# Reordering the stage ahead of the first exponential: dense work, slices and the maxima's rows

## Chip, cores and metric

The kernel runs on one core of one Trainium2 chip. The metric is the device time of one execution in microseconds, lower is better.

## The reference

One transformer block with adaptive layer norm. S is 2048 tokens, D is 512, 32 heads of width 16, F is 1792. All is float32.

```
mod = silu(c) @ w_mod                       # six rows of D: sa ca ga sb cb gb
h = layernorm(x) * (1 + ca) + sa
q, k, v = split(h @ wqkv)                   # 32 heads of 16
x = x + ga * (softmax(q k^T * 16**-0.5) v) @ wo
h = layernorm(x) * (1 + cb) + sb
a = h @ w1 + b1
x = x + gb * (a * tanh(softplus(a))) @ w2   # Mish
```

## The kernel before

**Precision.** A dense product is done three times (`mm3`), with each operand split into a high part and a low part: high by high, and the two mixed ones. A weight slice of `wqkv` is brought in by `slice_load` (an SP transfer into one buffer), then parted by `slice_split`: the high copy on ACT (`hi_copy`, L91), the low difference on POOL (`lo_sub`, L98). Kind 0 is queries, 1 keys, 2 values. Queries and keys come in four slices of 128 columns (eight heads each), values in two of 256.

**Setup.** Layer norm, its transposes and the first slices, in a loop over four blocks of 512 tokens. Its end is `constants()`: zero rows into the scratch of the queries (`qscr<-zer`) and of the values, and `b1`.

**Steps.** What follows is written out as steps t from -20 to 257; PRO is 20. Hooks stand at half-steps h: a hook of h = 2t is emitted at the start of step t, one of h = 2t+1 in its middle. A hook fixes an instruction's place in the order of its own engine or queue, and nothing else: each engine, and SP's DMA queue too, works down its own list in order and stops at the first instruction whose operands are missing.

**Steps -20 to -1** find the score maxima of the first group of four heads (and begin with the second). A step has two `max_pair`s: four half-height products on TensorE (L494) into two banks each of a ring of six, and two reductions on VectorE (L496). After them `whole_units` emits dense products out of a queue of units (`plan`): the values of the remaining token chunks (12 products of 256 columns a chunk), then key and query units of 12 products of 512 columns. A unit is taken when its half-step is at least that of its slice's split plus a margin. `CREDIT` says how many 512-column products a step is given. When the last unit of a plan entry is done, its `fin` orders the split of the slice two entries on and the load of the slice three entries on. A key or query unit ends with a copy to `qf` on ACT (L259), a split on POOL (L95, L98, two buffers) and, two half-steps later, writes to scratch by SP: three for queries (`qscr`, L269), two for keys (`kscr`, L273, L274).

**The maxima's rows.** The group's maxima are complete after step -5. In step -4 `max_rows` transposes them (L509), ACT and VectorE make rows of them (`mh` L511, `mt` L512), and the hook `put` at half-step -6 writes these into the query operand, `qa<-mt` (L518, four transfers). The score products of step 0 need them.

**Other transfers of the stage.** `early_prep` loads six parts of `w1`, POOL splits them, and SP writes them back to scratch (L1393, L1401), one each three half-steps. `load_pair` fetches queries and keys of two heads (L310, L319) at half-steps -22 and -8, `load_v` (L467) the values at -3.

**From step 0 on** a step has four score products (L529), each followed by an exponential on ACT (L532), four maxima products for the next group (L480) with their reductions (L482), up to eight half-height dense products (L136), which steps 0 and 1 have not, and eight products with the values (L547) for the step two back. They share the ring. The feed-forward part runs in the dense slots of later steps.

The functions that the diff touches:

Of the kernel before, what the change touches and what calls it, by code (L numbers as in the profile page):

```python
# [18 lines left out]
def adaln_block(ctx: ExitStack, tc: tile.TileContext, x, wqkv, wo, w1, b1, w2, c, w_mod, out):  # L19
# [8 lines left out]
    TB = 512  # L28
    NB = S // TB
# [3 lines left out]
    T = 16 * NIT  # L33
# [5 lines left out]
    PRO = 16 + LEAD  # L39
    CUT1, CUT2 = (0, 1), (2, 3)  # L40
    LOV = ((1,), (), (1, 3), (1, 3))
    PREP = 4
    CREDIT = 7.5
    HCAP = 10.0

    x = x[0]
# [39 lines left out]
    def dap(t, off, ap):  # L86
        return bass.AP(tensor=t.tensor, offset=t.offset + off, ap=ap)

    def hi_copy(eng, hi, src):
        if eng == "a":  # L90
            nc.scalar.copy(hi, src)  # L91
        elif eng == "v":
            nc.vector.tensor_copy(hi, src)
        else:
            nc.gpsimd.tensor_scalar(hi, src, 1.0, 0.0, op0=ALU.mult, op1=ALU.add)  # L95

    def lo_sub(eng, lo, src, hi):
        (nc.gpsimd if eng == "p" else nc.vector).tensor_sub(lo, src, hi.bitcast(F32))  # L98
# [43 lines left out]
    def pe_run():  # L142
        while pe_queue:
            mm_go(pe_queue.pop(0))
# [57 lines left out]
    def at(h, f):  # L202

        hooks.setdefault(h, []).append(f)
# [9 lines left out]
    pw = qkv.enter_context(tc.tile_pool(name="pp", bufs=1, side="right"))  # L214
# [12 lines left out]
    def slice_load(kind, i, pool=None, lp=None):  # L227
        w = P if kind < 2 else 2 * P
        raw = (pool or qp).tile([P, DK, w], F32, tag="raw" if pool is pw else "wr", name="wr", bufs=2 if lp else 1)
        o = kind * D + i * w  # L230
        nc.sync.dma_start(raw, wqkv[:, o:o + w].rearrange("(k p) m -> p k m", p=P))
        slices[kind, i] = raw

    def slice_split(kind, i, pool=None, eng="p", hi_eng="a"):
        raw = slices[kind, i]
        w = raw.shape[2]
        hi = (pool or qp).tile([P, DK, w], F32R, tag="wh", name="wh", bufs=2)
        lo = (pool or qp).tile([P, DK, w], F32R, tag="wl", name="wl", bufs=2)
        hi_copy(hi_eng, hi, raw)
        lo_sub(eng, lo, raw, hi)  # L240
        slices[kind, i] = (hi, lo)
# [84 lines left out]
    with ExitStack() as es:  # L326
# [5 lines left out]
        def load_x(t):  # L332
            xt = lp.tile([P, D], F32, tag="xt", name="xt", bufs=16)
            nc.sync.dma_start(xt, x[t * P:(t + 1) * P, :])
            xts.append(xt)
# [10 lines left out]
        slice_load(2, 0)  # L346
        for t in range(8, 16):
            load_x(t)
        slice_load(1, 1, pw)
        zer = lp.tile([P, TB], F32, name="zer")  # L350
        nc.gpsimd.memset(zer, 0.0)
        for i in range(NR):
# [12 lines left out]
        def stats_tb(tb):  # L365

            mv = lp.tile([P, 4, 2], F32, tag="ln_mv4", name="ln_mv4", bufs=2)
            rs = rss[tb] = lp.tile([P, 4, 4], F32, tag="ln_rs4", name="ln_rs4", bufs=3)
            for i in range(4):
                st_ = lp.tile([P, 6], F32, tag="ln_st", name="ln_st", bufs=4)  # L370
                nc.vector.bn_stats(out=st_, in_=xts[4 * tb + i])
                nc.vector.bn_aggr(out=mv[:, i, :], in_=st_)
            nc.gpsimd.tensor_scalar(rs[:, 0, :], mv[:, :, 1], 1.0, EPS, op0=ALU.mult, op1=ALU.add)
            nc.gpsimd.tensor_scalar(rs[:, 3, :], mv[:, :, 0], -1.0, 0.0, op0=ALU.mult, op1=ALU.add)
            nc.gpsimd.tensor_tensor(rs[:, 1, :], rs[:, 0, :], nhalf.to_broadcast([P, 4]), op=ALU.pow)
            nc.gpsimd.tensor_mul(rs[:, 2, :], rs[:, 3, :], rs[:, 1, :])

        def apply_tb(tb):
            rs = rss.pop(tb)
            for i in range(4):  # L380
                xt = xts[4 * tb + i]
                nc.scalar.activation(xt, xt, AF.Identity, scale=rs[:, 1, i:i + 1], bias=rs[:, 2, i:i + 1])
# [32 lines left out]
        def constants():  # L415
            for q4 in range(S // TB):
                nc.sync.dma_start(dap(qscr, 48 * S + q4 * TB, [[50 * S, H], [S, 2], [1, TB]]), zer[:64, :])
            nc.sync.dma_start(dap(vscr, VROW - 16, [[VROW, P], [P * VROW, G], [1, 16]]), zer[:, :16 * G])
            nc.sync.dma_start(b1c, b1.rearrange("(f p) -> p f", p=P))

        def unit(fin):
            pe_run()
            fin()

        for tb in range(NB):
            if tb + 2 < NB:
                stats_tb(tb + 2)
            if tb == 0:
                slice_split(2, 0, eng="v")
            parts = []  # L430
            for kind in (1, 0) if tb == 0 else (1,):
                fin = qk_unit(kind, 0, tb, "ring")
                parts.append((pe_queue[2 * DK:], fin))
                del pe_queue[2 * DK:]
                pe_run()
            if tb in (1, 2):
                for kc in (2 * tb - 2, 2 * tb - 1):
                    unit(v_unit(0, kc, "ring"))
            if tb + 1 < NB:
                tr_tb(tb + 1, CUT1)  # L440
            for late, fin in parts:
                pe_queue.extend(late)
                unit(fin)
            if tb + 1 < NB:
                tr_tb(tb + 1, CUT2)
            if tb + 2 < NB:
                apply_tb(tb + 2)
            if tb == 0:
                for pp in range(2):
                    load_q(pp, 48)  # L450
            for pp in range(2):
                load_k(pp, tb)
        constants()
        slice_split(1, 1)


    kq2 = ctx.enter_context(tc.tile_pool(name="kq2", bufs=1))
# [713 lines left out]
    cur = {"left": [], "fin": None, "part": []}  # L1171

    def queue(ready, make):
        units.append((ready, make))
# [22 lines left out]

    def whole_units(h, credit):

        while credit > 0:  # L1200
            if not cur["left"]:
                if not units or h < units[0][0]():
                    return
                cur["tag"] = "acc" if cur.get("tag") == "ms" else "ms"
                cur["fin"] = units.pop(0)[1](cur["tag"])
                cur["left"] = list(pe_queue)
                pe_queue.clear()
            m = cur["left"].pop(0)
            mm_go(m)
            credit -= m[0].shape[-1] / TB  # L1210
            if not cur["left"]:
                at(h + 1, lambda fin=cur["fin"]: fin(h + 1))
                cur["fin"] = None
# [7 lines left out]
    def step(t):  # L1221
# [4 lines left out]
        if t < 0:  # L1226
# [10 lines left out]
            for f in ats.pop(t, []):  # L1237
                f()
            whole_units(2 * t + 1, CREDIT)
            do_specials(2 * t + 1)  # L1240
# [83 lines left out]
    def do_specials(h):  # L1324
        if specials and h >= specials[0][0]():
# [2 lines left out]
            at(h + 1, lambda: fin(h + 1))  # L1328


    plan = [(-PRO, 2, 0, range(4, 16)), (-PRO, 1, 1, range(NB)), (-PRO, 0, 1, (0,)), (-PRO, 1, 2, range(NB)),
            (-PRO, 0, 2, (0,)), (0, 2, 1, range(16)), (0, 1, 3, range(NB)), (0, 0, 3, (0,))]
    plan += [(56, 0, ct, (1, 2, 3)) for ct in range(4)]
    split_at = {0: -2 * PRO - 4, 1: -2 * PRO - 4}

    def planned(i, a, tag):
        _, kind, sl, args = plan[i]
        unit = v_unit(sl, a, tag) if kind == 2 else qk_unit(kind, sl, a, tag)

        def fin(h):  # L1340
            if a == args[-1]:
                if i + 2 < len(plan):
                    d = 4 if h > 0 else 1
                    at(h + d, lambda: slice_split(*plan[i + 2][1:3], hi_eng="p" if h > 0 else "a"))
                    split_at[i + 2] = h + d
                if i + 3 < len(plan):
                    at(h + (7 if h > 0 else 2), lambda: slice_load(*plan[i + 3][1:3]))
            unit(h)
            if (kind, sl, a) == (2, 0, NKC - 1):
                at(max(0, h + 2), lambda: first_mods(max(0, h + 2)))  # L1350
            if i + 1 == len(plan) and a == args[-1]:
                mst["qkv"] = h // 2 + 3
        return fin
# [23 lines left out]
        queue_mod(j)  # L1377
    for i, (t0, _, _, args) in enumerate(plan):
        for a in args:
            queue(lambda i=i, t=t0: max(2 * t, split_at.get(i, 4 * T) + 4), lambda tag, i=i, a=a: planned(i, a, tag))  # L1380

    preps = [(w1scr[f], w1[:, f * P:(f + 1) * P].rearrange("(k p) m -> p k m", p=P), None) for f in range(FT)]
    preps += [(woscr[k], wo[k * P:(k + 1) * P, :], 0) for k in range(DK)]
# [4 lines left out]
    def early_prep(i, h):  # L1388

        scr, src, _ = preps[i]  # L1390
        lo, hi = [ap.tile([P, TB], F32R, tag=f"p{(1, 3, 0, 2)[i % 4]}", name="ep", bufs=4 - i % 4 // 2) for _ in range(2)]
        raw = lo.bitcast(F32)
        nc.sync.dma_start(raw.rearrange("p (k m) -> p k m", m=P), src)  # L1393

        def split():
            hi_copy("p", hi, raw)
            lo_sub("p", lo, raw, hi)

        def put():
            for v, part in enumerate((hi, lo)):  # L1400
                nc.sync.dma_start(scr[:, v, :], part.bitcast(F32))  # L1401

        at(h + 7, split)
        at(h + 10, put)

    for i in range(EARLY):
        at(3 * i - 34, lambda i=i: early_prep(i, 3 * i - 34))

    def start_preps(h, i=EARLY, turn=0, puts=()):

# [24 lines left out]
    for qb in range(NB - 1):  # L1435
        t0 = 32 * G * (qb + 1) + 16
# [15 lines left out]
    t = T + 2  # L1452
# [32 lines left out]
```

## Time and profile before

| | us |
|---|---|
| median of 3 runs | 1699.01 |
| lowest, highest | 1698.46, 1699.34 |
| profiled execution | 1697.49 |
| span of its trace | 1695.7 |
| TensorE busy in the span | 1672.8 |
| steps -20 to -1 begin | 50.6 |
| first score product begins | 105.40 |

In rows of the timeline the columns are start, length, engine, line, operation, tiles and count; a bracket at the end gives the idle time before it and what ended it. In rows of the windows they are the window, its length, the busy time of PE, PEld, DVE, ACT and POOL with their counts, the granted TensorE clock as a share of full speed, the share of DMA engines in use, and GB/s. PE is TensorE, DVE is VectorE, ACT is ScalarE, POOL is GpSimd, SPq is SP's DMA queue.

### The profile page before, as it was taken

The page shows a single profiled execution, that of the slowest core. Times are in us where ns is not written, and L with a number is a line of the kernel's source. Part 1 is how long each engine was busy: PE and PEld are TensorE (multiplying, and loading weights), DVE is VectorE, ACT ScalarE, POOL GpSimd, SP SyncE. Part 2 cuts the span into 40 slices and gives each one's busy share as a digit, 9 for nine tenths or more (in the row PEclk, how much of TensorE's full clock was granted, in tenths as well). Part 3 has the DMA queues.
Part 4 walks back from the last instruction along what each step waited for, and adds up shares of the span by engine and source line. Part 5 has one row for each costly group of instructions (what it writes and reads, how often), then busy time and mean ns, then how long its engine had stood idle before and what let it go on. Part 6 is the DMA issues. An engine that isn't in the chain of part 4 may idle for free.

```text
span 1695.7 us, 33728 instructions
## 1 busy us (share of the span) xinstructions
PE 1672.8 (99%) x12406; PEld 924.7 (55%) x12406; DVE 1437.8 (85%) x2370; ACT 1358.3 (80%) x2612; POOL 820.1 (48%) x838
## 2 busy tenths in 40 slices
PE   7999999999999999999999999999999999999999
PEld 5755665555445455555555455555555455555587
DVE  6888888888899888888889898888889988884378
ACT  6247777777778988888888998888888988888674
POOL 6456223665413464655423564555323564555442
PEclk9999999999999999999999999999999999999999
DMA  6887546777755342534355434434354433433261
GB/s 234 237 274 193 135 127 185 232 218 212 229 170 140 100 107 75 136 80 126 81 155 148 117 74 98 134 72 134 84 142 128 130 93 77 143 107 128 77 230 62
DMA packets 114029, 238.44 MB, mean 141 GB/s; under 512 B 23824, under 2 KB 49424, under 8 KB 107912
## 3 DMA queue, kind: packets, MB, share of 16 engines
q1 hardware_dynamic: 113864, 236.28, 49.3%
q8 instruction: 98, 1.61, 0.4%
q14 instruction: 67, 0.55, 0.1%
HBM read 179.95 MB, written 51.44 MB: 136 GB/s over the span
## 4 chain that ended last, share of the span: by engine, by line
PE 91%; DVE 4%; ACT 2%; DMA 2%; issue 0%; SPq 0%; POOL 0%; ACTq 0%; DVEq 0%
PE bk L547 29%; PE ring L529 23%; PE ring L480 20%; PE bk L136 9%; PE bk L129 3%; PE ring L1156 2%; DVE mx L482 2%; PE ring L129 2%; ACT pr L532 1%; DMA xt<-in_A_x 1%; PE ring L494 1%; DMA qa<-mt 1%; PE ring L859 0%; PE ring L509 0%; DVE hf L392 0%
## 5 line engine op out<-in xcount | busy, mean ns | idle before, releaser
L482 DVE TENSOR_REDUCE mx<-ring 128x1 f32<-128x512 f32 x1968 | 1223.0, 682 | 153.1 <-PE ring L480 137.4
L532 ACT ACTIVATE pr<-ring 128x512 f32<-128x512 f32 x2048 | 1078.3, 602 | 209.1 <-PE bk L136 121.1
L480 PE MATMUL ring<-ka,qa 64*128 64x512 f32 x1968 | 818.8, 430 | 1.6 <-ACT pr L532 1.1
L529 PE MATMUL ring<-qa,ka 64*128 64x512 f32 x2048 | 760.8, 403 | 5.4 <-DMA qa<-mt 2.6
L547 PE MATMUL bk<-pr,vg 128*32 128x512 f32 x4096 | 545.1, 604 | 0.0
L480 PEld LDWEIGHTS ring<-ka,qa 64*128 64x128 f32 x1968 | 351.2, 184 | 327.8 <-DVE mx L482 251.0
L529 PEld LDWEIGHTS ring<-qa,ka 64*128 64x128 f32 x2048 | 374.1, 184 | 199.0 <-DVE mx L482 114.7
L136 PE MATMUL bk<-h,w 64*128 64x512 f32 (+1 forms) x1080 | 278.9, 391 | 0.0
L136 PE MATMUL bk<-w,a_h 64*128 64x512 f32 x632 | 210.6, 413 | 0.0
L136 PEld LDWEIGHTS bk<-h,w 64*128 64x128 f32 x1080 | 178.3, 184 | 9.5 <-ACT pr L532 1.5
L547 PEld LDWEIGHTS bk<-pr,vg 128*32 128x32 f32 x4096 | 80.7, 108 | 136.2 <-issue 126.6
L136 PE MATMUL bk<-w,a_l 64*128 64x512 f32 x316 | 124.1, 393 | 0.0
L136 PEld LDWEIGHTS bk<-w,a_h 64*128 64x128 f32 x632 | 107.0, 184 | 2.2
L915 POOL TENSOR_TENSOR y<-yd,y 128x512 f32<-128x512 f32 x44 | 56.9, 1294 | 89.4 <-ACT yd L914 84.5
L749 POOL TENSOR_SCALAR qq<-ee 128x512 f32<-128x512 f32 x25 | 15.6, 624 | 169.3 <-ACT ee L743 169.3
L765 POOL TENSOR_TENSOR qq<-qq,rr 128x512 f32<-128x512 f32 x42 | 54.3, 1292 | 83.4 <-ACT rr L759 83.3
L751 POOL TENSOR_TENSOR hb<-hb,ee 128x512 f32<-128x512 f32 x42 | 54.2, 1291 | 82.3 <-DVE ee L747 80.4
L136 PE MATMUL bk<-w,o_hl 64*128 64x512 f32 x288 | 79.1, 405 | 0.0
L98 POOL TENSOR_TENSOR a_l<-hb,a_h 128x512 fp32r<-128x512 f32 x53 | 72.1, 1361 | 4.4
L136 PEld LDWEIGHTS bk<-w,a_l 64*128 64x128 f32 x316 | 58.3, 184 | 2.4
L136 PE MATMUL bk<-h_h,wl 64*128 64x512 f32 x168 | 57.7, 425 | 0.0
L95 POOL TENSOR_SCALAR qh<-qf 128x512 fp32r<-128x512 f32 x27 | 16.8, 622 | 82.8 <-ACT qf L259 56.3
(210 smaller groups left out, 1909.0 us busy)
## 6 DMA issues: line engine op xcount, KB each, us to landing
ka<-kscr SPq DMA_DIRECT2D x124, 384.0 KB
w<-w2scr SPq DMA_DIRECT2D x56, 512.0 KB
w<-w1scr SPq DMA_DIRECT2D x46, 512.0 KB
vg<-vscr SPq DMA_DIRECT2D x32, 552.0 KB
qa<-qscr SPq DMA_DIRECT2D x124, 100.0 KB
kscr<-qh SPq DMA_DIRECT2D x16, 512.0 KB
qscr<-qh SPq DMA_DIRECT2D x32, 256.0 KB
w2scr<-hl SPq DMA_DIRECT2D x14, 512.0 KB
```

The lines of the kernel that those rows point to most:

```text
L98: (nc.gpsimd if eng == "p" else nc.vector).tensor_sub(lo, src, hi.bitcast(F32))
L129: nc.tensor.matmul(acc, l, r, start=start, stop=stop)
L136: i = nc.tensor.matmul(acc, l[64 * g:64 * g + 64], r[64 * g:64 * g + 64], start=start and not then, stop=bool(stop and then))
L480: nc.tensor.matmul(pm, qt[64 * s:64 * s + 64, qs * P:(qs + 1) * P], kt[64 * s:64 * s + 64, kb * TB:(kb + 1) * TB], start=True, stop=True)
L482: nc.vector.tensor_reduce(out=mxs[n][:, s, 4 * j + qs, kb:kb + 1], in_=pm, op=ALU.max, axis=AX.X)
L529: nc.tensor.matmul(p_, kt[64 * s:64 * s + 64, kc * P:(kc + 1) * P], qt[64 * s:64 * s + 64, :], start=True, stop=True)
L532: e = nc.scalar.activation(pr, p_, AF.Exp, scale=SCALE)
L547: nc.tensor.matmul(accs[n][32 * h:32 * h + 32, :], vgs[n][:, o:o + 32], pts.pop((t, h)), start=(kc == 0), stop=(kc == 15))
L751: (nc.vector if tail else nc.gpsimd).tensor_mul(hb, hb, ee)
L765: nc.gpsimd.tensor_mul(qq, qq, rr)
L915: nc.gpsimd.tensor_add(y[i], yd, y[i])
L1156: nc.tensor.matmul(po[i // 2][:, i % 2, :], l[:, s], w[:, r, :], start=(f == 0 and j == 0), stop=(f == FT - 1 and j == 2))
```

## The change

It does five things. The queries' unit of the second slice goes ahead of the key units of that slice in `plan`, so it is the query slice that is loaded and split in the setup. `whole_units` carries what a step was over or under its credit on to the next step, and the credit is 7.4. The split and the load of some plan entries get fixed half-steps (`LATE_SPLIT`, `LATE_LOAD`, by plan entry counted from 0) instead of following the end of an earlier entry, and units ahead of step 0 may start two half-steps after their split, not four. The constants are written ahead of the setup's loop and not behind it. The early parts of `w1` start three half-steps earlier.

```
-    CREDIT = 7.5
+    CREDIT = 7.4
+    LATE_SPLIT = {3: -8, 4: 4}
+    LATE_LOAD = {3: -15, 4: -4, 5: 9}
...
-        slice_load(1, 1, pw)
+        slice_load(0, 1, pw)
...
+        constants()
         for tb in range(NB):
...
-        constants()
-        slice_split(1, 1)
+        slice_split(0, 1)
...
     def whole_units(h, credit):
 
-        while credit > 0:
+        cur["owed"] = cur.get("owed", 0) + credit
+        while cur["owed"] > 0.49:
             if not cur["left"]:
                 if not units or h < units[0][0]():
+                    cur["owed"] = 0
                     return
...
-            credit -= m[0].shape[-1] / TB
+            cur["owed"] -= m[0].shape[-1] / TB
...
-    plan = [(-PRO, 2, 0, range(4, 16)), (-PRO, 1, 1, range(NB)), (-PRO, 0, 1, (0,)), (-PRO, 1, 2, range(NB)),
+    plan = [(-PRO, 2, 0, range(4, 16)), (-PRO, 0, 1, (0,)), (-PRO, 1, 1, range(NB)), (-PRO, 1, 2, range(NB)),
             (-PRO, 0, 2, (0,)), (0, 2, 1, range(16)), (0, 1, 3, range(NB)), (0, 0, 3, (0,))]
...
-                    at(h + d, lambda: slice_split(*plan[i + 2][1:3], hi_eng="p" if h > 0 else "a"))
-                    split_at[i + 2] = h + d
+                    split_at[i + 2] = LATE_SPLIT.get(i + 2, h + d)
+                    at(split_at[i + 2], lambda: slice_split(*plan[i + 2][1:3], hi_eng="p" if h > 0 else "a"))
                 if i + 3 < len(plan):
-                    at(h + (7 if h > 0 else 2), lambda: slice_load(*plan[i + 3][1:3]))
+                    at(LATE_LOAD.get(i + 3, h + 7), lambda: slice_load(*plan[i + 3][1:3]))
...
-            queue(lambda i=i, t=t0: max(2 * t, split_at.get(i, 4 * T) + 4), lambda tag, i=i, a=a: planned(i, a, tag))
+            queue(lambda i=i, t=t0: max(2 * t, split_at.get(i, 4 * T) + (2 if t < 0 else 4)), lambda tag, i=i, a=a: planned(i, a, tag))
...
-        at(3 * i - 34, lambda i=i: early_prep(i, 3 * i - 34))
+        at(3 * i - 37, lambda i=i: early_prep(i, 3 * i - 37))
```

## The prediction

> **What bounds the kernel now.** I read the page first: busy shares, then the chain that ended last.
>
> ```profile
> span 1695.7 us, 33728 instructions
> PE 1672.8 (99%) x12406; PEld 924.7 (55%) x12406; DVE 1437.8 (85%) x2370; ACT 1358.3 (80%) x2612; POOL 820.1 (48%) x838
> ```
>
> TensorE sets the time nearly everywhere, so the change can only help where TensorE waits or runs slowly. The chain in order of time shows the one long step that is not compute near the first exponential.
>
> ```profile
> 101.08 4.19 DMA qa<-mt
> 105.40 0.47 PE ring L529
> ```
>
> These are the maxima's rows, the last operand of the first score product. The next view is TensorE's timeline: an undisturbed step of the opening stage (four maxima products L494, then eight dense products L129), and then its last three steps.
>
> ```profile
> 87.92 0.73 PE L494 MATMUL ring<-ka,qa 64*128 64x512 f32 x4
> ...
> 88.92 1.09 PE L129 MATMUL bk<-h_h,wh 128*128 128x512 f32 x4
> 89.85 0.85 PE L129 MATMUL bk<-h_h,wl 128*128 128x512 f32 x3
> 90.63 0.73 PE L494 MATMUL ring<-ka,qa 64*128 64x512 f32 x4
> ...
> 93.34 0.73 PE L494 MATMUL ring<-ka,qa 64*128 64x512 f32 x4
> ...
> 96.08 0.73 PE L494 MATMUL ring<-ka,qa 64*128 64x512 f32 x4
> 96.74 0.50 PE L129 MATMUL bk<-h_l,wh 128*128 128x512 f32 x1
> 97.17 0.51 PE L494 MATMUL ring<-ka,qa 64*128 64x512 f32 x2
> 97.90 0.50 PE L494 MATMUL ring<-ka,qa 64*128 64x512 f32 x2 [0.22 <-DVE mx L496]
> 98.33 1.21 PE L129 MATMUL bk<-h_h,wh 128*128 128x512 f32 x4
> 99.55 1.19 PE L129 MATMUL bk<-h_h,wl 128*128 128x512 f32 x4
> 100.67 0.73 PE L494 MATMUL ring<-ka,qa 64*128 64x512 f32 x4
> 101.34 1.19 PE L129 MATMUL bk<-h_l,wh 128*128 128x512 f32 x4
> 102.37 1.07 PE L129 MATMUL bk<-h_h,wh 128*128 128x512 f32 x4
> 105.40 0.47 PE L529 MATMUL ring<-qa,ka 64*128 64x512 f32 x1 [1.96 <-DMA qa<-mt]
> ```
>
> A step is 90.63 - 87.92 = 2.71 us. Four dense products take 89.85 - 88.92 = 0.93 us, 0.2325 each; eight make 1.86, so the four maxima products and the changeovers cost 0.85 a step. Step -3 (from 96.08) holds one dense product only: the next unit was not ready by the planner's count. VectorE then becomes the bound (the 0.22), and the next eight products are spread out. Step -2's lows wait for POOL's split, below. Then 1.96 us pass with nothing to do.
>
> **Part one: dense work per step.** Counting by the code, before does 15 half-width (256) products a step (credit 7.5), or eight whole ones, until the 144 of the values are done; then 3 in step -11, 8 in each of -10 to -4, 1, 8, 8: 76 whole products. After carries the remainder of 7.4 over: 2 in step -11, then 7, 8, 7, 8, 7, 7, 8, 7, 8, 7 in steps -10 to -1. That is 76 again: 12 for the queries, 48 for the second key slice, 16 of the third. Both kernels thus leave the same 32 products of the third slice to the main loop, and from step 2 on take units in the same order. So nothing is moved into or out of the stage; only holes can close. Readiness holds by the count: the second key slice is split at half-step -19, ready at -17, and first wanted at -17; the third is ready at -6 and wanted at -5.
>
> From 96.08 to the first exponential's product is 9.32 us. The work in it is 3 x 0.85 + 17 x 0.2325 = 6.50. With no hole and no wait, step 0 starts at 96.08 + 6.50 = 102.58: **2.82 us** gained. VectorE must keep up:
>
> ```profile
> 96.17 0.33 DVE L512 SCALAR_TENSOR_TENSOR mt<-mh,lows,ring 32x128 fp32r<-32x128 f32 x1
> 96.62 6.95 DVE L496 TENSOR_REDUCE mx<-ring 128x2 f32<-128x1024 f32 x6
> ```
>
> Six reductions in 6.95 us make 2.32 a step. A seven-product step takes TensorE 0.85 + 1.63 = 2.48, so it still leads by 0.16, and the mean step leads by more.
>
> **Part two: the rows' place in SP's queue.**
>
> ```profile
> 98.21 1.28 POOL L98 TENSOR_TENSOR wl<-wr,wh 128x512 fp32r<-128x512 f32 x1
> 99.53 0.38 SPq L231 DMA_DIRECT2D wr<-in_A_wqkv  x1
> 99.96 0.50 SPq L273 DMA_DIRECT2D kscr<-qh  x1
> 101.08 2.96 SPq L518 DMA_DIRECT2D qa<-mt  x4
> ```
>
> The rows are ready at 96.17 + 0.33 = 96.50 but go out at 101.08, behind a slice load that waits for POOL to empty its buffer (98.21 + 1.28) and a key write. After puts that load at half-step -4 and the rows at -6, alone. Step -4 begins 4 x 0.85 + 30 x 0.2325 = 10.38 before step 0, at 92.2; the rows were ready 3.16 after their step's start (93.34 to 96.50), so at 95.4. From issue to use they took 105.40 - 101.08 = 4.32, so they land near 99.7, **2.9 us before** step 0 wants them.
>
> Still ahead of the rows in SP's queue are the queries' three writes, the last early weights, two key writes and the fourth pair's load. The second of those key writes (key block 1) needs POOL's split of its own, and POOL's buffer for that is free only when the queries' writes have landed:
>
> ```profile
> 31.92 5.58 DMA qscr<-ql
> 102.47 0.62 POOL L95 TENSOR_SCALAR qh<-qf 128x512 fp32r<-128x512 f32 x1 [2.97 <-DMA kscr<-qh]
> ```
>
> The queries' unit ends in step -9, near 80.6 (I count back as above). With a split of 0.62 + 1.28 behind other POOL work its writes leave by about 85 and land by 91 at the 5.58 they once took. Key block 1 is then split by 93 and written by 94, ahead of 95.4. POOL and SP have a little over a microsecond to spare there, and the rows 2.9 behind that.
>
> **Part three: the clock.** After the wait, two steps follow without dense work.
>
> ```profile
> 104.60:108.00 3.40, 2.41 (x12) 1.55 (x12) 2.06 (x4) 2.56 (x6) 3.04 (x3) 1.00 0.73 197
> 108.00:111.40 3.40, 3.40 (x16) 2.85 (x17) 3.40 (x7) 2.54 (x5) 0.00 (x0) 0.51 0.77 237
> 105.94 7.27 DVE L482 TENSOR_REDUCE mx<-ring 128x1 f32<-128x512 f32 x12 [2.37 <-PE ring L480]
> 113.95 0.69 DVE L482 TENSOR_REDUCE mx<-ring 128x1 f32<-128x512 f32 x1 [0.74 <-PE ring L480]
> 112.42 1.06 PE L547 MATMUL bk<-pr,vg 128*32 128x512 f32 x8
> ```
>
> The granted clock (the column ahead of the DMA share) is 0.51 for 3.4 us: at most 1.7 us of TensorE's time. Little of it is on the path, because VectorE works without a pause from 105.94 through twelve reductions, 0.606 each. Six banks hold three maxima, so the twelfth maximum needs the ninth reduction done: 105.94 + 5.45 = 111.4. Two slots of 0.23 later the first product with the values could start, at 111.9 rather than 112.42: 0.5. The other reading is VectorE's own wait for TensorE afterwards, 0.74. I take **0.6**, between the two, with 0 and 1.7 as the ends.
>
> The Trainium skill (TensorE: Matmul & The Clock Gate, "What's actually happening") lets the clock fall after at least one idle window of about 3.4 us. The trace differs: 1.96 us of idling, then sparse products, had it fall. By the page's rule this gap never cost the clock, and the sum would be 2.82 alone, 1696.2, the weak end of the forecast's own range.
>
> **Part four: what is moved at no cost.** The constants' transfers go from the end of the setup to before its loop.
>
> ```profile
> 18.01 0.38 SPq L231 DMA_DIRECT2D wr<-in_A_wqkv  x1
> 28.05 0.38 SPq L273 DMA_DIRECT2D kscr<-qh  x1
> 60.37 2.50 SPq L417 DMA_DIRECT2D qscr<-zer  x4
> 66.48 5.30 POOL L460 MEMSET ka<- 128x2048 f32 x3 [13.26 <-DMA b1c<-in_B_b]
> ```
>
> They took 66.48 - 60.37 = 6.1 us from first issue to landing. SP has nothing to issue between 18.4 and 28.05, every x tile is queued earlier, and 18.4 + 6.1 = 24.5 is ahead of 28.05: no cost. If they were slower by more than 3.5 us, the key write of the first block would be late by the rest. POOL's memset no longer waits for them, which relieves the early weights' splits, but TensorE waits for none of these before step -2.
>
> The fourth slice's split (queries, third head group) moves to half-step 4, where ACT's cast stands ahead of step 2's exponentials:
>
> ```profile
> 103.82 0.62 ACT L91 CAST wh<-wr 128x512 fp32r<-128x512 f32 x1 [4.94 <-DMA wr<-in_A_wqkv]
> 105.91 4.04 ACT L532 ACTIVATE pr<-ring 128x512 f32<-128x512 f32 x8 [0.84 <-PE ring L480]
> ```
>
> Twelve exponentials at 0.505 are 6.1 us beside VectorE's 7.27, so 1.2 us are free for the 0.62. Its load is issued near 99 and took 103.82 - 99.53 = 4.3, done by 103.3; ACT wants it near 106. Without that cover each late microsecond would cost one. The fifth load (half-step 9) is wanted at 28 only.
>
> **Sum.** 2.82 + 0.6 = 3.4 us off. The profiled run took 1697.49 (span 1695.7 and 1.8 around it), 1.5 below the median 1699.01; I take the gain off the median: **1695.6**. A run of this kernel spreads by 0.9 us, and about 0.2% (3.4 us) is what a measurement can tell from no change: the forecast lies on that bound.
>
> **Rivals.**
> 1. *The rows still wait* (0.11). Key block 1's write or a filled DMA queue holds them; if they come when step 0 is due plus 1.96, only the hole closes: 0.87 off, 1698.1. For it: thin slack at key block 1. Against: the 2.9 us.
> 2. *The clock falls anyway* (0.10). If the two sparse, VectorE-paced steps and not the gap bring it down, a half-clock stretch of 3.4 us comes later, where TensorE is the bound, costing between 0 and 1.7: 1696.2 to 1697.9. For it: the clock fell 2.6 us after the gap. Against: without the gap they fill a window better than 104.6 to 108.0 was filled. The same page ("A second HAM failure mode") describes clocks that fall from many short pauses.
> 3. *Slower: the queries' writes block POOL* (0.06). They hold the buffer key block 1 needs; behind that on POOL stands the third slice's split, on SP the rows, and TensorE stops for both. Landing is followed by 1.9 of split and 1.1 of key write (99.96 to 101.08), so their 5.58 would have to grow: from 7.4 us the rows are delayed, from 10.3 step 0 is, beyond 13.7 the 3.4 are lost, and at 17.1 it is 3.4 slower, 1702.4. Against: the transfers before the rows are fewer than before (two key writes and not four).
> 4. *The change does not fill the steps* (0.03). If a slice is not ready by the count the credit is dropped and a hole remains, near 1699.
>
> **How the numbers follow.** The forecast has 0.70; its own range is 1694.5 (2.82 + 1.7) to 1696.2 (2.82 alone). Its clock term decides on which side of the bound it falls; the interval from 0.58 to 1.7 is faster, so I split it 0.47 and 0.23. Rival 2 gives 0.03 faster, 0.07 same; rivals 1 and 4 are the same, rival 3 slower. Faster 0.50, same 0.44, slower 0.06. The range goes from 1693.9 (the low end less the runs' 0.55) to rival 1's 1698.1.
>
> **What would show it.** Steps of seven and eight dense products with no single one; qa<-mt issued near 95.4 and landed before L529; no idle on TensorE ahead of the first L529, which starts near 102.6; granted clock 1.00 from there on; first L547 near 109.0. I am wrong if L529 still names qa<-mt, if a 0.5 clock reappears, or if TensorE waits for a wl, wh or a copy between steps -9 and 2.

## The result, and the profile after

| | before | after |
|---|---|---|
| median of 22 runs, us | 1698.49 | 1695.56 |
| lowest, highest | 1696.86, 1700.38 | 1694.41, 1698.78 |
| profiled execution | 1697.49 | 1696.57 |
| first score product begins | 105.40 | 102.70 |
| first product with the values begins | 112.42 | 109.45 |

The medians differ by 2.93 us, or 0.17%; the ratio of the runs is 0.9984, with a 95% interval of 0.9978 to 0.9990. It is a gain, and it lies within the 0.2% that the prediction called its bound. The forecast was 1695.6.

The page of the changed kernel has the same shape as before's, with 2.6 us less on TensorE.

```profile
PE 1670.2 (99%) x12406; PEld 920.9 (54%) x12406; DVE 1442.4 (85%) x2370; ACT 1358.0 (80%) x2612; POOL 820.1 (48%) x838
```

TensorE's timeline shows the last four steps before the first exponential. After's lines stand two below before's: L496 are the maxima products, L131 the dense ones, L531 the scores, L549 the products with the values.

```profile
92.09 0.73 PE L496 MATMUL ring<-ka,qa 64*128 64x512 f32 x4
92.94 0.28 PE L511 MATMUL ring<-ident,mm 128*32 128x128 f32 x1
...
95.02 0.73 PE L496 MATMUL ring<-ka,qa 64*128 64x512 f32 x4
95.69 0.73 PE L131 MATMUL bk<-h_h,wl 128*128 128x512 f32 x2
96.26 1.09 PE L131 MATMUL bk<-h_l,wh 128*128 128x512 f32 x4
97.19 0.40 PE L131 MATMUL bk<-h_h,wh 128*128 128x512 f32 x1
97.51 0.73 PE L496 MATMUL ring<-ka,qa 64*128 64x512 f32 x4
...
101.67 1.09 PE L131 MATMUL bk<-h_h,wh 128*128 128x512 f32 x4
102.70 0.49 PE L531 MATMUL ring<-qa,ka 64*128 64x512 f32 x1
...
109.45 1.06 PE L549 MATMUL bk<-pr,vg 128*32 128x512 f32 x8
```

The step with a single dense product is gone (seven here, from 95.69 to 97.51), and no bracket stands on the first L531: the rows had landed. SP's queue has them where the prediction put them, at 95.45, ahead of the slice's load:

```profile
93.19 0.41 SPq L276 DMA_DIRECT2D kscr<-ql  x1
95.45 2.79 SPq L520 DMA_DIRECT2D qa<-mt  x4
98.34 0.40 SPq L233 DMA_DIRECT2D wr<-in_A_wqkv  x1
```

The windows show the clock at full speed where before's was halved. Their columns are as in the prediction, and VectorE's row shows what sets the pace there:

```profile
104.60:108.00 3.40, 3.34 (x18) 1.80 (x17) 3.40 (x6) 3.40 (x8) 0.93 (x2) 1.00 1.01 359
108.00:111.40 3.40, 3.30 (x26) 1.46 (x24) 2.95 (x6) 2.10 (x5) 1.82 (x2) 1.00 1.04 360
103.26 7.26 DVE L484 TENSOR_REDUCE mx<-ring 128x1 f32<-128x512 f32 x12 [0.15 <-PE ring L482]
```

The first product with the values thus comes 112.42 - 109.45 = 2.97 us earlier; 0.11 of that is the setup, which ended earlier in this execution (50.59 and 50.48). The two profiled executions differ by only 0.9, in part because this run of after loses time again near 385 us, at the rows of a later group, where the profiled run of before has no wait (its next one for rows is 0.59 us, at 433 us):

```profile
385.25 0.46 PE L531 MATMUL ring<-qa,ka 64*128 64x512 f32 x1 [1.87 <-DMA qa<-mt]
```

Its size changes from kernel to kernel (0 to 1.9 us in the profiles of this case), so the medians are the better measure of the whole, and the opening stage is read by itself below.

### The profile page after: what moved, and what is told of

Read it like the earlier page. It is cut to its first block, busy times and chain, and to the rows that moved or that the text cites. A ratio compares the mean times of both kernels' runs of the same rounds, so it can differ in the third digit from the quotient of the medians.

```text
span 1694.6 us, 33732 instructions
## 1 busy us (share of the span) xinstructions
PE 1670.2 (99%) x12406; PEld 920.9 (54%) x12406; DVE 1442.4 (85%) x2370; ACT 1358.0 (80%) x2612; POOL 820.1 (48%) x838
## 4 chain that ended last, share of the span: by engine, by line
PE 91%; DVE 4%; ACT 2%; DMA 2%; issue 0%; POOL 0%; SPq 0%; ACTq 0%; DVEq 0%; POOLq 0%
PE bk L549 29%; PE ring L531 22%; PE ring L482 20%; PE bk L138 10%; PE bk L131 3%; PE ring L131 2%; DVE mx L484 2%; PE ring L1158 2%; ACT pr L534 1%; DMA xt<-in_A_x 1%; PE ring L496 1%; DMA qa<-mt 0%; PE ring L861 0%; PE ring L511 0%; PE ring L138 0%
## 5 line engine op out<-in xcount | busy, mean ns | idle before, releaser
L531 PE MATMUL ring<-qa,ka 64*128 64x512 f32 x2048 | 760.4, 403 | 4.7 <-ACT pr L534 2.2
L549 PE MATMUL bk<-pr,vg 128*32 128x512 f32 x4096 | 545.0, 604 | 0.0
L531 PEld LDWEIGHTS ring<-qa,ka 64*128 64x128 f32 x2048 | 373.6, 184 | 198.6 <-DVE mx L484 114.0
L549 PEld LDWEIGHTS bk<-pr,vg 128*32 128x32 f32 x4096 | 80.7, 108 | 136.2 <-issue 126.6
```

Of the source, the lines that this page charges most:

```text
L531: nc.tensor.matmul(p_, kt[64 * s:64 * s + 64, kc * P:(kc + 1) * P], qt[64 * s:64 * s + 64, :], start=True, stop=True)
L549: nc.tensor.matmul(accs[n][32 * h:32 * h + 32, :], vgs[n][:, o:o + 32], pts.pop((t, h)), start=(kc == 0), stop=(kc == 15))
```

## The experiments

Theory one was the prediction's: the rows' new place in SP's queue takes away the wait of 1.96, the even steps close the hole, the clock follows the wait, and the constants' move is only cover. The rival that came out of the first runs: the constants' early place does nearly all of it. One table holds what each run but the last gave. "To scores" and "to values" run from the first maxima product (50.2 to 50.9 us in these runs) to the first score product and to the first product with the values, in the one execution of each kernel that was profiled. "Half clock" is how long the granted clock stood near 0.5 after the first score. The last two columns compare with the kernel before's runs on the same chip. In fences below that hold rows of several engines, the rows between them are left out.

| kernel | to scores | to values | TensorE's waits of over 1 us near step 0 | half clock | median less before's | ratio, 95% |
|---|---|---|---|---|---|---|
| before | 54.81 | 61.83 | 1.96 | 3.4 | | |
| after | 52.22 | 58.98 | none | 0 | -2.93 | 0.9978 to 0.9990 |
| before, rows at once | 52.66 | 61.35 | 1.77 | 3.4 | -0.07 | 0.9992 to 1.0010 |
| before, rows at once and cast late | 53.24 | 61.67 | 2.31 | 3.4 | -0.70 | 0.9988 to 1.0005 |
| after, rows late | 53.53 | 60.52 | 1.26 | 3.4 | -1.26 | 0.9985 to 1.0003 |
| after, uneven steps | 53.58 | 60.10 | none | 0 | -1.39 | 0.9988 to 1.0006 |
| after, keys first | 52.72 | 59.24 | none | 0 | -3.23 | 0.9974 to 0.9992 |
| after, constants late | 55.96 | 64.96 | 2.08, 1.35, 1.87 | 6.8 | +2.03 | 1.0003 to 1.0021 |
| before, constants early | 52.56 | 59.29 | none | 0 | -2.59 | 0.9973 to 0.9991 |
| the same, GpSimd held | 55.82 | 63.47 | 2.75 | 6.8 | -0.20 | 0.9986 to 1.0005 |
| after, rows at once for all groups | 52.20 | 58.96 | none | 0 | -3.26 | 0.9975 to 0.9993 |

**The rows at once, alone.** Before, with one edit to the first group's rows:

```
-        at(2 * (16 * n + 16 - PRO) + 2, put)
+        if n == 0:
+            put()
+        else:
+            at(2 * (16 * n + 16 - PRO) + 2, put)
```

> The kernel before, with one edit: the first group's rows are put into SP's queue right after they are made, ahead of the slice load and the key write of half-step -6. The hole in step -3 stays. Theory (hole 0.87, wait 1.96, clock the rest): the rows go out near 97 and land near 101.5, the first score product starts near 103.4 with no wait for them, the clock stays at 1.00, the first product with the values starts near 110.2; 2.0 to 2.3 us off the median. Rival (the wait and the hole are the same thing: with the rows early, TensorE would still stand until VectorE has caught up): first score later than 104.4, gain under 1.

The rows went out at 97.06, ahead of the slice's load, and landed in time for a first score at 103.09. Yet nothing was won: 1698.38 against 1698.45, where 2.0 to 2.3 us were expected. ACT's and TensorE's timelines show what took their place.

```profile
100.40 0.39 SPq L231 DMA_DIRECT2D wr<-in_A_wqkv  x1
104.09 0.62 ACT L91 CAST wh<-wr 128x512 fp32r<-128x512 f32 x1 [5.50 <-DMA wr<-in_A_wqkv]
105.17 4.03 ACT L535 ACTIVATE pr<-ring 128x512 f32<-128x512 f32 x8
105.82 0.50 PE L532 MATMUL ring<-qa,ka 64*128 64x512 f32 x1 [1.77 <-ACT pr L535]
```

The fourth slice's load now stood behind the rows. ACT's cast of that slice stands ahead of the first exponential and waited for it, so the exponentials began at 105.17 and the ring's banks came free late. The wait moved from SP to ACT, almost at its old size.

**The rows at once, and that cast out of the way.** The edit above, and the fourth slice's load and split at the places that the change gives them:

```
-                    split_at[i + 2] = h + d
+                    split_at[i + 2] = 4 if i == 2 else h + d
...
-                    at(h + (7 if h > 0 else 2), lambda: slice_load(*plan[i + 3][1:3]))
+                    at({4: -4, 5: 9}.get(i + 3, h + (7 if h > 0 else 2)), lambda: slice_load(*plan[i + 3][1:3]))
```

> The kernel before, with the first group's rows put at once, and the fourth slice moved as in after: its load at half-step -4, its split at 4, the fifth load at 9. The hole stays, the constants stay late, steps stay uneven. Theory: the rows alone gained nothing because ACT's cast, ahead of the first exponentials, waited for the load that the rows had pushed back; with the cast behind them, the first score is near 103.1, no 1.8 us wait for ACT follows, the first product with the values is near 110.0, the clock stays at 1.00; 2.0 to 2.5 us off before's median. Rival (ACT is held by the copy behind POOL, not by the cast): a wait of over 1 us for ACT after the first scores stays.

```profile
103.59 0.62 POOL L95 TENSOR_SCALAR qh<-qf 128x512 fp32r<-128x512 f32 x1 [4.02 <-DMA kscr<-qh]
105.59 0.58 ACT L259 COPY qf<-bk 128x512 f32<-128x512 f32 x1 [6.63 <-POOL ql L98]
106.73 0.60 PE L532 MATMUL ring<-qa,ka 64*128 64x512 f32 x1 [2.31 <-ACT pr L535]
```

The rival's sign came: a wait of over 1 us for ACT, and 0.70 us off the median, not told apart from none. Now ACT's copy of a finished key block is what stands ahead of the exponentials. It waits for POOL to empty `qf`, and POOL for a key write to land. Three things (rows, cast, copy) hang on one late chain of key writes, and taking one out lets the next decide.

**The rows later.** After, with the first group's rows three half-steps later:

```
-        at(2 * (16 * n + 16 - PRO) + 2, put)
+        at(2 * (16 * n + 16 - PRO) + (2 if n else 5), put)
```

> The kernel after, with one edit: the first group's rows go into SP's queue at half-step -3 instead of -6, behind the fourth slice's load, two key writes' worth of SP time and the values' load. Everything else of the change stays. Theory: rows out near 101, landed near 105.4, first score product 2.7 us later than after's 102.70, and most of the gain is gone (1.5 to 3 us slower than after). If the idle time is what brings the clock down, a 0.5 clock of 3.4 us appears within 4 us of the first score. Rival (the gain comes from the even steps, the rows' place is incidental): within 1 us of after.

They went out at 98.37, not near 101, and TensorE waited 1.26 us for them (first score at 103.85). The clock halved again for 3.4 us. The place is worth 60.52 - 58.98 = 1.5 us once the rest is in order, and the medians, each less its before, differ by 1.7; their intervals overlap.

**Uneven steps.** After, with the old credit and nothing carried over:

```
-    CREDIT = 7.4
+    CREDIT = 7.5
...
-        cur["owed"] = cur.get("owed", 0) + credit
-        while cur["owed"] > 0.49:
+        cur["owed"] = credit
+        while cur["owed"] > 0:
```

> The kernel after, with one edit: the old rule of the credit (7.5 a step, overshoot not carried over), so 15 half-width or 8 whole products in every step. By the count the stage then does 83 whole products and not 76, and the main loop 7 fewer. Theory: the order of the slices alone closes the hole; the 7 products lengthen the stage by 7 x 0.2325 = 1.6, first score near 104.3, no wait for rows; the main loop gives almost nothing back, since a step with dense products there takes about 2.84 us and one without 2.73: 1.2 to 1.7 us slower than after. Rival (evenness itself is worth the gain: uneven steps bring holes): a stall of TensorE for VectorE in the stage, first score after 105. Second rival (work is only moved): same median as after.

As expected: no wait and no drop of the clock, and the first score 1.36 us later for seven more dense products (the trace has 83 in the stage, after's 76). Steps 0 and 1 are as sparse as before, so sparse steps alone don't lower the clock.

**Keys first.** After, with the old order of units (the key slice is loaded and split in the setup, the third split at half-step -7, and the credit is 7.5, still carried over):

```
-    CREDIT = 7.4
-    LATE_SPLIT = {3: -8, 4: 4}
+    CREDIT = 7.5
+    LATE_SPLIT = {3: -7, 4: 4}
...
-        slice_load(0, 1, pw)
+        slice_load(1, 1, pw)
...
-        slice_split(0, 1)
+        slice_split(1, 1)
...
-    plan = [(-PRO, 2, 0, range(4, 16)), (-PRO, 0, 1, (0,)), (-PRO, 1, 1, range(NB)), (-PRO, 1, 2, range(NB)),
+    plan = [(-PRO, 2, 0, range(4, 16)), (-PRO, 1, 1, range(NB)), (-PRO, 0, 1, (0,)), (-PRO, 1, 2, range(NB)),
```

> The kernel after with the keys' units of the second slice ahead of the queries' unit again (in the plan, the setup's load and its split). Two numbers have to follow, or a query slice of the main loop would miss its place: credit 7.5, still carried over, and the third slice's split at half-step -7. By the count the stage then does 78 whole products, two more than after (0.5 us). Theory: the order decides what stands ahead of the rows in SP's queue; here a third key write does, which waits for POOL, so the rows leave near 99 instead of 95.45 and land near 103.5; the third slice's lows are late as well. First score 103.2 to 104.2 with a wait of up to 1 us, 0.7 to 2 us slower than after. Rival (the order is incidental once the steps are even and the constants early): first score at 103.2 without a wait, 0.5 us slower than after.

The rows went out at 95.93, not near 99, and no wait came back: the first score is at 103.20, as the rival said, and the time is not told apart from after's (-3.23 and -2.93). The queries' unit need not go first.

**The constants late.** After, with the constants back behind the setup's loop:

```
-        constants()
         for tb in range(NB):
...
+        constants()
         slice_split(0, 1)
```

> The kernel after, with one edit: the constants' transfers go back behind the setup's loop. Theory: POOL's memset waits for them again until about 66 and the early weights run later, but TensorE waits for nothing of that; first score within 0.3 us of 102.70 and the median within 0.5 us of after. Rival (SP's queue and the DMA engines were relieved by the move, and that is what made the rows early): the rows land after step 0 is due, first score after 103.5.

The expectation was wrong by a lot. This is the largest effect of any single part: 1700.48, slower than before, with the first score at 106.60. The timelines of POOL, SP's queue and TensorE:

```profile
66.06 5.30 POOL L462 MEMSET ka<- 128x2048 f32 x3 [12.81 <-DMA b1c<-in_B_b]
82.39 0.62 POOL L97 TENSOR_SCALAR qh<-qf 128x512 fp32r<-128x512 f32 x1
82.52 4.42 SPq L1405 DMA_DIRECT2D w1scr<-ep  x4
96.44 0.63 POOL L97 TENSOR_SCALAR qh<-qf 128x512 fp32r<-128x512 f32 x1 [8.14 <-DMA qscr<-qh]
99.55 0.50 PE L131 MATMUL bk<-h_h,wh 128*128 128x512 f32 x1 [2.08 <-ACT qf L261]
106.60 0.47 PE L531 MATMUL ring<-qa,ka 64*128 64x512 f32 x1 [1.35 <-DMA qa<-mt]
109.44 0.79 PE L531 MATMUL ring<-qa,ka 64*128 64x512 f32 x1 [1.87 <-ACT pr L534]
```

POOL begins the split of the queries' block at 82.39, 0.79 us later than in after (81.60). But four writes of early weights (L1405), held up with POOL, now fill SP's queue ahead of the queries' writes, which leave at 88.30 (82.25 in after) and hold POOL for 8.14 us. That is the mechanism of the prediction's third rival, with TensorE stopped for a copy, for the rows and for an exponential in turn.

**The constants early, alone.** The kernel before, with that one move and nothing else:

```
+        constants()
         for tb in range(NB):
...
-        constants()
         slice_split(1, 1)
```

> The kernel before, with one edit: the constants' transfers go ahead of the setup's loop. Theory after the run with the constants late: in the order of before, no queries' write stands ahead of the second key block, so the relief is worth little by itself: the hole in step -3 stays, the rows still stand behind the slice load; first score within 1 us of 105.40, median 0 to 1 us better. Rival (the constants are the main cause of all that follows): first score below 104, over 2 us off.

It takes 1696.69, a gain of 2.6 us where at most 1 was expected, and its interval covers that of after. The steps are still uneven, but the first product with the values comes 2.54 us sooner after the stage's start than in before, and the clock stays at 1.00. GpSimd and SP:

```profile
52.87 5.30 POOL L460 MEMSET ka<- 128x2048 f32 x3
65.24 0.63 POOL L95 TENSOR_SCALAR ep<-ep 128x512 fp32r<-128x512 f32 x1 [7.07 <-DMA ep<-in_B_w]
68.74 1.47 SPq L1401 DMA_DIRECT2D w1scr<-ep  x2
80.96 0.81 SPq L1401 DMA_DIRECT2D w1scr<-ep  x2
81.42 0.62 POOL L95 TENSOR_SCALAR qh<-qf 128x512 fp32r<-128x512 f32 x1 [0.95 <-ACT qf L259]
82.07 0.37 SPq L273 DMA_DIRECT2D kscr<-qh  x1
89.56 0.62 POOL L95 TENSOR_SCALAR qh<-qf 128x512 fp32r<-128x512 f32 x1 [0.29 <-ACT qf L259]
95.14 1.28 POOL L98 TENSOR_TENSOR wl<-wr,wh 128x512 fp32r<-128x512 f32 x1
98.00 3.10 SPq L518 DMA_DIRECT2D qa<-mt  x4
```

The same places in the kernel before:

```profile
71.75 0.63 POOL L95 TENSOR_SCALAR ep<-ep 128x512 fp32r<-128x512 f32 x1
72.41 1.72 SPq L1401 DMA_DIRECT2D w1scr<-ep  x2
81.73 0.62 POOL L95 TENSOR_SCALAR qh<-qf 128x512 fp32r<-128x512 f32 x1 [0.86 <-ACT qf L259]
83.91 0.82 SPq L1401 DMA_DIRECT2D w1scr<-ep  x2
84.96 0.37 SPq L273 DMA_DIRECT2D kscr<-qh  x1
91.94 0.62 POOL L95 TENSOR_SCALAR qh<-qf 128x512 fp32r<-128x512 f32 x1 [2.34 <-DMA kscr<-qh]
```

POOL's fills of the three new key buffers no longer wait for the constants (13.26 us in the prediction's row). Its first split of an early weight moves from 71.75 to 65.24, the first write of one from 72.41 to 68.74, the first key write from 84.96 to 82.07, the third slice's split from 98.21 to 95.14, and the rows from 101.08 to 98.00. The transfers stand in the same order in SP's queue as before, some three microseconds sooner. The first key block shows the link: its split begins at almost the same time in both (81.73 and 81.42), but its write stands behind a weight write that leaves at 83.91 in the one and at 80.96 in the other. With the late write POOL then waits 2.34 us for a buffer before the third key block's split; with the early one it doesn't wait for a write there.

**GpSimd held, the constants early.** Two causes were left in that move: POOL's wait, and the constants' own transfers on SP and in the DMA engines at 60 to 66 us. This kernel has the constants early and lets POOL do the fills eleven times:

```
-    for t in ka[2:]:
+    for t in ka[2:] * 3 + ka[2:4]:
```

> The kernel before with the constants early, and GpSimd's three fills of the new operand buffers done 11 times in place of 3: GpSimd is held from 52.9 for 11 x 1.77 = 19.4 us, to 72.3, about where the late constants held it in the kernel before (71.75). The constants' transfers stay early. Theory one (the late constants cost their time by keeping GpSimd from the first late weights' splits, whose writes then lie beside the keys' writes): the third slice's split is late again by some 3 us (98 and not 95.1), the rows go out near 101 and not 98.0, the first score product starts near 105.4 with about 2 us of wait, the clock shows a stretch of 0.5 after it, and the time is that of the kernel before, within 0.8 us. Rival (the constants' own transfers, on SP's queue and in the DMA engines at 60 to 66 us, cost the time): rows out at 98.0, first score near 102.9, the time 2.6 us under the kernel before, as with the constants early alone.

```profile
52.90 19.29 POOL L460 MEMSET ka<- 128x2048 f32 x11
85.59 0.37 SPq L273 DMA_DIRECT2D kscr<-qh  x1
101.04 2.81 SPq L518 DMA_DIRECT2D qa<-mt  x4
106.15 0.47 PE L529 MATMUL ring<-qa,ka 64*128 64x512 f32 x1 [2.75 <-DMA qa<-mt]
```

The rows leave at 101.04, against 101.08 in the kernel before; the wait and the half clock are back, and the time is before's (-0.20). So it is through GpSimd that the late constants cost their time: holding it takes back the whole gain, with the transfers still early. The copy of before isn't exact, since GpSimd writes memory here while it only waited there, and the profiled execution (0.9 us over its median) is 1.0 us longer to the first score than before's.

**The rows at once for all groups.** After, with `put()` in place of `at(2 * (16 * n + 16 - PRO) + 2, put)`:

> The kernel after, with one edit: every group's rows go into SP's queue right after they are made, not at the next half-step behind what was registered there. It is tried as a better version: after's trace still waits 1.9 us for rows once, at 385. Theory: nothing changes before the first score; if SP's order caused the later wait it goes, and up to 1 us comes off the median. Rival (there the rows are ready late and wait in filled DMA engines, not in SP's queue): within 0.5 us of after.

It takes 1696.02, not to be told from after, and the later wait near 385 is still 0.5 us.

**Later places for writes.** After, with one threshold lowered in a helper that keeps SP's queue clear ahead of each group's rows:

```
     def clear(h):
 
-        return h if h < 60 or h % 32 < 25 else h - h % 32 + 34
+        return h if h < 60 or h % 32 < 20 else h - h % 32 + 34
```

> The changed kernel, with one threshold of the weights' places lower (25 to 20 half-steps of 32), so that fewer weight transfers stand in SP's queue ahead of each later group's rows. Theory one: the wait of about 0.5 to 1.9 us for group 6's rows near 385 us goes, nothing takes its place, and the time is 0.5 to 1.5 us under the changed kernel's, 1694.1 to 1695.1 for a before of 1698.5. Rival: other transfers take the places left free, another group's rows or keys wait, and the time is within 0.4 us of the changed kernel's or up to 2 us over it. The opening stage is the same in both: first score product at 102.7.

It takes 1724.62, slower than before by 1.5% (1.0139 to 1.0166), where a gain or at most 2 us of loss was expected. The helper also places the scratch writes of key and query units, and these hold POOL's two buffers:

```profile
355.79 0.62 POOL L97 TENSOR_SCALAR qh<-qf 128x512 fp32r<-128x512 f32 x1 [20.41 <-DMA qscr<-qh]
358.94 0.79 PE L138 MATMUL bk<-h_h,wh 64*128 64x512 f32 x1 [5.80 <-ACT qf L261]
```

It is the opening stage's chain once more: a write put off by a few steps is a buffer held, a split not done, and TensorE stopped.

Two parts of the change were not run by themselves: the three half-steps that the early weights were brought forward, and the fixed places of the splits and loads. What all parts but the constants add together is the small difference between the constants early alone and after.

## Why the prediction was right, and where it was not

**The time and the places were right.** First score 102.70 (102.58 forecast), rows out 95.45 (95.4) and in time, no stall, clock 1.00, first product with the values 109.45 (109.0). The sum of 3.4 came out as 2.9. That it came so near is partly luck: the part that earned most of it, the constants' move, was in the change for no gain.

**Part one** counted rightly (the traces have 76 dense products in both stages), but the hole was not closed by the even steps alone. The first score came 2.70 us earlier, not 2.82, and 0.11 of that is the earlier start of the stage: in step -4 TensorE waits for VectorE's last maxima before it can transpose them (L511 at 92.94), 0.2 us that the count of products left out. What the new order and the even steps add to the early constants is small: the stage is 0.3 us shorter by the table, and the medians (1696.69 on one chip, 1695.56 on another) are not told apart. Within the changed kernel the carried credit makes the stage 1.1 us shorter, by the uneven one: that order has no empty step, so eight products in every step come to 83 and not 76. The medians differ by 1.5, with intervals that overlap.

**Part two named the wrong cause.** It gave the 1.96 us to the rows' new place. In the kernel before, going out at once brought at most half a microsecond. What delayed the rows delayed the load behind them and the copies too, and an earlier place for one of these is no use while the chain of key writes is late. With the constants early, the old place was good enough.

**Part three** was right that without the wait the clock would stay up. The term came out nearer 0.3 than 0.6 (2.97 less 2.70): VectorE sets the pace from 103.26 on (twelve reductions in 7.26 us), as the prediction said. Rival 2, that sparse steps alone bring the clock down, fell with every kernel that had no wait; all of them have the same two steps.

**Part four failed at one sentence**: "TensorE waits for none of these before step -2". The 13.26 us in POOL's row were called relief for the early weights' splits and priced at nothing. No one instruction of TensorE waits for them, but SP's queue runs in order: the splits feed weight writes, these stand ahead of the key writes, and the key writes hold POOL's buffers and go ahead of the rows. Put back, the constants cost 5 us; moved alone, they give 2.6. That the move was not free could have been seen by following who waits behind each late step, not only whom TensorE names.

**Rival 3** was judged rightly for this kernel: the margin at key block 1 held, with 0.56 us of waiting for the queries' writes.

```profile
90.95 1.30 POOL L100 TENSOR_TENSOR ql<-qf,qh 128x512 fp32r<-128x512 f32 x1 [0.56 <-DMA qscr<-ql]
```

But the reason given against it, fewer transfers ahead of the rows, was not enough to protect it. The early constants were needed too: without them it happens, and the kernel is slower than before.

## What to carry to other kernels

Before moving the step that a wait names, ask what made that step late, and follow the idle time of a "cheap" engine through every queue that works in order. Here a 13 us pause on GpSimd at 53 us, with TensorE 99% busy beside it, set the wait on TensorE at 103. Test the parts of a change one at a time in both directions: here the part that was put down as free gave nearly all of the gain.

## What the hardware showed that was not expected

The clock does not go by the length of one pause. It halved after waits of 1.26 to 2.75 us around the first scores, in every kernel that had one there, and by the page (the Trainium skill, TensorE: Matmul & The Clock Gate, "What's actually happening"), which asks for an idle window of about 3.4 us, none of these would have done it. But the 1.87 us wait at 385 us in after left the clock at 1.00. The windows, cut at multiples of 3.41 us from the last rise of the clock, differ in the number of products (in brackets behind PE's busy time). First GpSimd held, then after:

```profile
103.30:106.70 3.40, 0.65 (x6) 0.56 (x6) 0.24 (x2) 1.25 (x3) 3.20 (x4) 1.00 0.87 294
106.70:110.10 3.40, 3.40 (x15) 2.29 (x12) 3.40 (x6) 3.40 (x7) 1.52 (x2) 0.51 0.69 217
```

```profile
380.87:384.28 3.41, 2.52 (x22) 1.15 (x18) 2.48 (x4) 2.56 (x5) 0.82 (x2) 1.00 0.55 193
384.28:387.70 3.42, 2.44 (x22) 1.48 (x22) 1.91 (x4) 1.95 (x4) 2.78 (x3) 1.00 0.86 200
```

In before, the window ahead of the fall held 12 products in 2.41 us (in the prediction). After's window of 384.28 has as little busy time, 2.44, but 22 products, and no fall followed. Each fall began where such a window ended and lasted one or two of them.

But neither the busy time nor the number of products decides by itself. Two earlier windows of before have less of both, and the clock stayed at 1.00:

```profile
46.60:50.01 3.41, 2.28 (x8) 1.42 (x8) 3.38 (x5) 0.04 (x1) 1.26 (x1) 1.00 0.81 286
101.21:104.63 3.42, 2.23 (x10) 1.43 (x8) 2.36 (x3) 0.77 (x2) 2.01 (x3) 1.00 0.88 316
```

Their products are full-height dense ones (128 rows) but for two at the start of the second, while those ahead of before's fall are half-height (64 rows). Counted by height, the windows without a fall hold 8 and 9 whole products, and the one ahead of the fall 6. That the work done in a window decides, not its longest pause, fits these, but not cleanly: the kernel with the constants early has a window from 104.02 with 14 half-height products, 7 whole ones, in 3.35 us, and no fall followed. No kernel was made to test it, and it stays open.
